# A bias pipeline run one group ahead, DMA zeros, fillers by length and joined multiplies in an attention kernel on one core

## The chip, the core and the metric

The kernel runs on one core of a Trainium2 chip. The metric is device time in microseconds (us), a median of several executions. Engines: PE (TensorE), PEld (its weight loads), DVE (VectorE), ACT (ScalarE), POOL (GpSimd), SP (SyncE). In the views, L411 is line 411 of that kernel, `<-` names what ended the idle time before an instruction, and PEclk is the clock granted to PE, 1.00 being full speed. The profiled executions were all fast. Three of the timed ones were slow (one of vrag_after, one of oldattn_loads_raw6, and one of the kernel before in the set with 404.1); the ratios leave them out, the medians and highest times don't.

A ratio is the mean time of one kernel's fast runs over that of the other's of the same rounds, so it is not quite the ratio of the medians beside it. The same kernel before took 404 to 405 us on some chips and 414 to 418 us on others, so times are compared only within one set of runs, which shared a chip.

## The reference

Attention for 8 batches, 8 heads, 576 positions and head size 64, with a bias that a small network computes from the distance of two positions; then each of the 4608 rows goes through the expert that its domain id names.

```python
x = (log1p(abs(i - j)) / log1p(max(i, 1)))[..., None]
bias = relu(x @ w1 + b1) @ w2            # hidden size 32, one bias for each head
scores = scale * q @ k.T + bias          # 576 x 576 for each batch and head
attn = exp(scores - max) / sum           # softmax
rows = (attn @ v)                        # 4608 rows of 512
for e in range(8):                       # 512 -> 1024 -> 512
    out[domain_id == e] = relu(rows[domain_id == e] @ w1[e]) @ w2[e]
```

## The kernel before

It has four stages: bias tables (0 to 69 us), attention (to 239), a hand-over in which rows are scattered to their experts and read back transposed (to 253), and the experts (to the end).

**Bias.** Nine groups of 16 hidden rows. DVE and ACT make the rows `hr`, PE multiplies them by the second layer, ACT evicts the result from PSUM as exp(bias) into `biasM`. Rows and outputs of one group stand next to each other in the program:

```python
for ib in range(9):
    hrl = []
    for k16 in range(16):                         # first layer: 16 rows
        ...                                       # on ACT for k16 in (3, 8, 13), else on DVE
        if ib > 0 or k16 > 7:
            next(route, None)                     # one step of the routing, on DVE
    for p in {5: (4, 0), 7: (1, 2)}.get(ib, ()):  at.take(0, p)
    for p in {4: (4, 0), 6: (1, 2), 8: (3,)}.get(ib, ()):  at.transposes(0, p)
    for jcs in ((0, 1), (2, 3), (4,)):            # second layer and evictions
        ...
at.make_vext(0)
at.take(0, 3)
```

**Attention.** A batch is 21 *units* of scores, counted from 0 here; each is 128 keys by 1024 scores at most. A unit is: score matmuls on PE, one exponential on ACT, and for most units a multiply by exp(bias) on DVE. Units of key block 3 (`RAW`, four a batch) instead get the bare bias added by two more PE matmuls, and cost DVE nothing. Between units PE gets *fillers*: a quarter of a PV product (`av`), or the transposes of a later batch. DVE copies the transposes (`take`), divides each finished PV product by its sums (`norm`) and copies V once a batch (`make_vext`). The next PV product reuses the same PSUM buffer, so it waits for the norm.

```python
while n < B * NU or av:
    b, ui = divmod(n, NU)
    new = self.scores(b, units[ui])               # PE scores, ACT exponential
    self.weight(job)                              # DVE multiply of the unit before
    job = new
    if b < B - 2 and ui == 1:   self.load_qk(b + 2); self.load_v(b + 2)   # load_qk loads the last rows too
    if b < B - 2 and ui == 9:   self.load_vrag(b + 2)
    if b < B - 1 and ui == 8:   self.make_vext(b + 1)
    budget = 4 if b >= B else 2 if n % 3 == 2 else 1
    while budget and (av or tr):                  # fillers: 1, 1, 2, 1, 1, 2, ...
        ...
```

**Zeros and ones.** POOL zeroes the ragged V tiles (`vrag`, for the last 64 keys), writes their columns of ones, zeroes the tiles of last rows (`last`), then issues its loads, and after them zeroes a tile with which one DMA of 9.25 MB fills the buffer that the rows are scattered to.

```python
for t in self.vrag:
    nc.gpsimd.memset(t, 0.0)
    nc.gpsimd.memset(t[0:64, :, 64:65], 1.0)
    nc.gpsimd.memset(t[64:128, :, 129:130], 1.0)
for t in self.last:
    nc.gpsimd.memset(t, 0.0)
...
at.start()                                        # the first loads
nc.gpsimd.memset(zv[:, :, 0:DM], 0.0)
nc.sync.dma_start(out=x_dram..., in_=zero.to_broadcast(...))
_phase_bias(tc, G, route, at)
```

The softmax here doesn't subtract the row's maximum and nothing guards it: scores larger than these inputs give would overflow.

## Time and profile before

The execution that was profiled took 404.8 us (span 403.1); the median given with it was 415.3.

| stage | from, us | to, us | what limits it |
|---|---|---|---|
| bias tables | 0 | 68.9 | DVE at first (busy for 10.9 of 11.0 us, 15 to 26), then ACT and PE in turn (37.6 and 32.4 of 42.0 us, 26 to 68) |
| attention | 68.9 | 238.7 | ACT (busy for 157.4 of 170.0 us), with PE close behind it (156.1) |
| hand-over | 238.7 | 252.7 | DMA and first transposes (PE waits 10.0 us for `xT`) |
| experts | 252.7 | 403.1 | PE (busy for 141.3 of 142.0 us, 253 to 395) |

"From" of attention is the start of the first score exponential, "to" the end of the last one; the experts begin with their first matmul. The eight batches, from first exponential to first exponential, lasted 21.6, 21.1, 21.3, 21.4, 21.2, 21.2, 21.2 and 20.7 us. The part of the profile that groups instructions by line has the two kinds of units beside each other. A row is: line, engine, operation, out<-in, shapes and count; then busy us and mean ns of one; then the idle time before them and who ended it.

```profile
L488 DVE TENSOR_TENSOR e<-e,biasM 128x1024 f16<-128x1024 f16 x96 | 63.2, 685 | 7.4 <-ACT e L483 7.0
L455 PE MATMUL sc<-biasM,idn 128*128 128x512 f16 x64 | 19.0, 378 | 3.1 <-ACT e L483 3.0
```

There are 96 multiplies (12 a batch by this tile) and 64 RAW matmuls (two for each of 32 RAW units). The change trades the one for the other.

### The profile page before, as it was taken

How to read it: one execution, taken by the hardware profiler on the slowest of the kernel's cores; microseconds unless marked ns; L12 is line 12 of the kernel's file. 1: busy time of each engine (PE TensorE's matmuls, PEld its weight loads, DVE VectorE, ACT ScalarE, POOL GpSimd, SP SyncE). 2: the span in 40 equal slices, each digit the busy share in tenths (PEclk: the TensorE clock that was granted, in tenths of full speed). 3: DMA queues.
4: the chain of work that ended last, by engine and by line, in shares of the span. 5: the costliest groups of instructions: out<-in, count | busy, mean ns of one | idle time of the engine just before them, and what ended most of it. 6: DMA issues, size and time to landing. Idle time of an engine off the chain costs nothing. (4 is left out here: it accounts for less than half of the span.)

```text
span 403.1 us, 9609 instructions
## 1 busy us (share of the span) xinstructions
PE 339.1 (84%) x3986; PEld 216.7 (54%) x3986; DVE 232.9 (58%) x486; ACT 256.7 (64%) x315; POOL 171.6 (43%) x232
## 2 busy tenths in 40 slices
PE   0357778889998999999897960999999999999991
PEld 0346666455656565656564540556565564655650
DVE  7999992878888888979797762020302213031220
ACT  8468989899999999999999960325042341514320
POOL 8660006603927639367470804044626323041321
PEclk9999985999999999999999996699999999999997
DMA  0999947980699998999492733959999999130311
GB/s 4 157 189 399 388 168 96 150 105 21 125 191 177 171 191 154 189 189 150 92 151 68 128 90 94 162 119 222 172 215 213 218 224 221 37 116 13 115 52 68
DMA packets 86068, 60.51 MB, mean 150 GB/s; under 512 B 43398, under 2 KB 76166, under 8 KB 86024
## 3 DMA queue, kind: packets, MB, share of 16 engines
q0 software_dynamic: 55808, 45.12, 65.6%
q1 hardware_dynamic: 30216, 14.78, 15.1%
q8 instruction: 31, 0.51, 0.5%
q14 instruction: 13, 0.11, 0.1%
HBM read 61.93 MB, written 24.70 MB: 215 GB/s over the span
## 5 line engine op out<-in xcount | busy, mean ns | idle before, releaser
L483 ACT ACTIVATE e<-sc 128x1024 f16<-128x1024 f32 x168 | 157.5, 994 | 12.5 <-PE sc L458 7.5
L670 DVE COPY res<-ops 128x512 f32<-128x512 f32 x40 | 27.7, 691 | 122.3 <-PE ops L667 122.3
L712 ACT ACTIVATE hT<-hps 128x640 f16<-128x640 f32 x56 | 39.4, 704 | 81.9 <-PE hps L693 81.9
L693 PE MATMUL hps<-xT,w 128*128 128x320 f16 x512 | 73.6, 306 | 10.0 <-DMA xT<-fire_x 10.0
L671 POOL DMA_INDIRECT out_dram<-res,ids x40 | 39.8, 996 | 93.4 <-DVE res L670 82.7
L667 PE MATMUL ops<-w,hT 128*128 128x512 f16 x320 | 70.4, 379 | 0.0
L693 PEld LDWEIGHTS <-w 128*128 128x128 f16 x512 | 51.2, 100 | 32.3 <-issue 10.1
L488 DVE TENSOR_TENSOR e<-e,biasM 128x1024 f16<-128x1024 f16 x96 | 63.2, 685 | 7.4 <-ACT e L483 7.0
L458 PE MATMUL sc<-qkT 64*128 64x512 f16 x256 | 50.3, 388 | 6.2 <-ACT e L483 5.4
L667 PEld LDWEIGHTS <-hT 128*128 128x128 f16 x320 | 31.3, 98 | 36.5
L505 PE MATMUL pu<-vext,e 128*128 128x65 f16 x1024 | 50.5, 194 | 0.0
L178 DVE TENSOR_SCALAR hr<-L,slope,nb 128x576 f16<-128x576 f16 x115 | 45.2, 459 | 0.0
L505 PEld LDWEIGHTS <-e 128*128 128x128 f16 x1024 | 43.7, 98 | 1.8 <-issue 0.8
L563 POOL DMA_INDIRECT fire_x<-xt,posi x32 | 34.5, 1077 | 18.9 <-issue 6.8
L196 PE MATMUL eb<-W2BIG,hr 128*128 128x32 f16 x576 | 26.4, 193 | 13.9 <-ACT hr L175 10.2
L501 PE MATMUL pu<-vrag,e 128*128 128x130 f16 x128 | 28.9, 226 | 5.2 <-DVE xl L549 2.1
L196 PEld LDWEIGHTS <-hr 128*128 128x128 f16 x576 | 22.1, 116 | 18.0 <-ACT hr L175 12.2
L563 POOL DMA_INDIRECT fire_x<-xl,posi x8 | 8.7, 1083 | 48.9 <-issue 26.6
L458 PEld LDWEIGHTS <-qkT 64*128 64x128 f16 x256 | 13.7, 93 | 28.6 <-issue 20.7
L635 POOL DMA_DIRECT2D w<-in_moe_w_dram x32 | 25.0, 810 | 4.5 <-DMA w<-in_moe_w_dram 4.5
L501 PEld LDWEIGHTS <-e 128*128 128x128 f16 x128 | 12.4, 97 | 24.2 <-issue 12.4
L388 POOL DMA_DIRECT2D qn<-in_q_dram x8 | 7.7, 964 | 40.8 <-PE pt L415 38.2
(116 smaller groups left out, 399.1 us busy)
## 6 DMA issues: line engine op xcount, KB each, us to landing
w<-in_moe_w_dram POOLq DMA_DIRECT2D x32, 512.0 KB, 9.5
fire_x<-zero SPq DMA_DIRECT2D x1, 9252.0 KB
qn<-in_q_dram POOLq DMA_DIRECT2D x8, 512.0 KB, 10.7
kn<-in_k_dram POOLq DMA_DIRECT2D x8, 512.0 KB, 8.8
vst<-in_v_dram POOLq DMA_DIRECT2D x8, 512.0 KB, 10.4
out_dram<-res,ids POOLq DMA_INDIRECT x40, 4.3
last<-in_q_dram POOLq DMA_DIRECT2D x16, 32.0 KB, 7.7
last<-in_k_dram POOLq DMA_DIRECT2D x16, 32.0 KB, 7.2
```

Of the source, the lines that this page charges most:

```text
L178: nc.vector.tensor_scalar(out=hr, in0=G.L4[:, c0: c0 + S], scalar1=G.slope[:, m: m + 1], scalar2=G.nb1[:], op0=AO.mult, op1=AO.max)
L196: nc.tensor.matmul(out=eb[:, lj, 32 * k16: 32 * k16 + 32], lhsT=rap(hr, jc, [[4, 128]]), rhs=G.W2BIG[:, 0:32], start=True, stop=True)
L458: mm(out=sc[:, h2, :], lhsT=self.qkT[b, p][hs[h2], 1, 128 * c: 128 * c + 128], rhs=self.qkT[b, p][hs[h2], 0, :], start=not raw, stop=True)
L483: nc.scalar.activation(out=ef[:, 0:n], in_=sf[:, 0:n], func=AF.Exp, bias=0.0, scale=0.125)
L488: self.nc.vector.tensor_tensor(out=job[0], in0=job[0], in1=job[1], op=AO.mult)
L501: mm(out=self.pu[:, c // 2, o: o + 130], lhsT=er[:, p % 2, 128 * c: 128 * c + 128], rhs=vr[:, p, :], start=True, stop=False, skip_group_ch ...
L505: mm(out=self.pu[:, c // 2, o + 65 * h2: o + 65 * h2 + 65], lhsT=self.e[b, ("m", p, j)][:, h2, 128 * c: 128 * c + 128], rhs=vx[:, 2 * p + ...
L563: inst = self.nc.gpsimd.indirect_dma_start(out=self.x_dram[:, :], out_offset=bass.IndirectOffsetOnAxis(ap=self.G.posi[0:n, c:c + 1], axis= ...
L667: nc.tensor.matmul(out=ops_, lhsT=hT[:, fc, t0: t0 + 128], rhs=G.w.w2(e, fc), start=(fc == 0), stop=(fc == 7))
L671: inst = nc.gpsimd.indirect_dma_start(out=out[:], out_offset=bass.IndirectOffsetOnAxis(ap=idx.bitcast(I32), axis=0), in_=res[:], in_offset ...
L693: nc.tensor.matmul(out=hps[:, i, 0:HC], lhsT=G.w.w1(e, dc)[:, 128 * fc: 128 * fc + 128], rhs=xT[:, dc, HC * hf: HC * hf + HC], start=(dc = ...
L712: nc.scalar.activation(out=hT[:, fc, :].rearrange("p (a b) -> p a b", a=2), in_=first(e, xT, ((fc, 0), (fc, 1))), func=AF.Relu, bias=0.0, ...
```

## The change

The intent: let ACT make rows while PE multiplies the group before; free POOL of memsets, so that loads go out earlier; give PE fillers by the time that a unit leaves, not by count; join two units in one multiply; and have two RAW units a batch instead of four. The core of the diff, with cuts marked:

```diff
-RAW = (3,)
+RAW = {3: 4}                      # block 3, from head 4 on: 2 units a batch
...
-        for ib in range(9):
+        def hidden(ib):            # 16 rows, 24 of 144 on ACT; routing steps in groups 1 and 2
...
+        hrl = hidden(0)
+        at.ones()
+        for ib in range(9):
+            after = hidden(ib + 1) if ib < 8 else None
+            ...                    # transposes of pairs 4, 0, 1 only; V copy
+                for _ in route:    # at ib == 8: the rest of the routing
+                    pass
+            outputs(ib, hrl)
+            hrl = after
...
         for t in self.vrag:
-            nc.gpsimd.memset(t, 0.0)
-            nc.gpsimd.memset(t[0:64, :, 64:65], 1.0)
-            nc.gpsimd.memset(t[64:128, :, 129:130], 1.0)
+            nc.sync.dma_start(out=t..., in_=G.zero...)
...
+    def ones(self):
+        for t in self.vrag:
+            self.nc.vector.memset(t[0:64, :, 64:65], 1.0)
+            self.nc.vector.memset(t[64:128, :, 129:130], 1.0)
...
     def start(self):
-        self.load_qk(0) ... self.load_vrag(1)
+        for b in range(2):
+            self.load_qk(b)
+            self.load_v(b)
+            self.load_last(b)
+            self.load_vrag(b)
...
+        self.joined = {("l", 0): 0, ("l", 1): 1}
+        for p in range(4):
+            n = 4 if all(2 * p < RAW.get(c, H) for c in range(4)) else 2
+            self.joined.update({("m", p, c): c % 2 for c in range(n)})
...
+                room = min(room + (0.5 if units[ui][0] == "x" else 0.91) - cost(units[ui]), 0.7)
...
-            if b < B - 2 and ui == 1:
+            if b < B - 2 and ui == 3:
                 self.load_qk(b + 2)
+            if b < B - 2 and ui == 7:
                 self.load_v(b + 2)
+                self.load_last(b + 2)
...
-            budget = 4 if b >= B else 2 if n % 3 == 2 else 1
-            while budget and (av or tr):
+            while av or tr:
+                lag = 2 if b >= B - 1 else 3
+                if av and room >= 0.34 - 0.15 and not (...):
...
+                    room -= 0.34
+                elif tr and room >= 0.52 - 0.15 and n >= NU * (tr[0][0] - 1) + 1:
+                    transpose()
+                    room -= 0.52
...
-            nc.gpsimd.memset(zv[:, :, 0:DM], 0.0)
             nc.sync.dma_start(out=x_dram..., in_=G.zero.to_broadcast(...))   # now before the loads have landed
```

The zero tile is now set by DVE, early, and the fill is issued as soon as that is done.

## The prediction

> **What bounds the kernel now.** I read the page's slices first, then busy time by stretch, then the waits inside each stretch, then single instructions in order of time.
>
> ```profile
> core 0: us, PE busy (x) PEld busy (x) DVE busy (x) ACT busy (x) POOL busy (x), PEclk, DMA share, GB/s
> 15.00:26.00 11.00, 6.43 (x131) 5.43 (x131) 10.90 (x38) 5.46 (x9) 6.74 (x10) 1.00 1.55 189
> 26.00:68.00 42.00, 32.44 (x670) 28.73 (x668) 36.06 (x95) 37.58 (x61) 7.39 (x10) 0.87 0.87 259
> ...
> 132.00:154.00 22.00, 20.48 (x315) 13.13 (x313) 19.14 (x36) 20.34 (x22) 11.43 (x14) 1.00 1.26 195
> ...
> 239.00:253.00 14.00, 1.86 (x38) 1.56 (x39) 3.90 (x14) 0.00 (x0) 5.02 (x5) 0.70 0.33 84
> 253.00:395.00 142.00, 141.25 (x832) 82.29 (x830) 27.66 (x40) 45.06 (x64) 50.01 (x53) 0.98 0.74 149
> ```
>
> Stretch by stretch: bias tables to 68 us (DVE full to 26, then ACT the busiest), attention from 69 to 239 (PE, ACT and DVE all near full), a hole of 14 us at the hand-over, then the expert layers, in which PE is never free. The last, 142 us of the 403, is not edited; its gain is nil. So the change lives in the first 253 us.
>
> In the bias stretch the chain goes round between ACT and PE:
>
> ```profile
> engine line waited for: us in total, times, longest us
> ...
> ACT biasM L214 <- PE eb L196: 12.7, 8, 5.3
> PEld L196 <- ACT hr L175: 12.2, 19, 1.9
> ...
> PE eb L196 <- ACT hr L175: 10.2, 18, 1.8
> ```
>
> PE waits for the rows that ACT makes, ACT waits for PE before it can evict. From group 3 the first eviction of a group starts at 37.80, 43.44, 49.06, 54.69, 60.33, 65.97: a period of 5.63 us, which is three rows (2.38) + wait (0.47) + evictions (2.11 + 0.76). DVE shows as busy there, but its rows start every 0.34 us when unhindered, 13 of them 4.5 us: it has some 1 us of slack a group.
>
> In attention I took the starts of the score exponentials one by one. Undisturbed they follow at 0.90 to 0.92 us; 20 of those and the short one (0.3) make 18.6 us a batch. The batches in fact start at 111.64, 132.96, 154.40, 175.61: 21.2 to 21.4 us. Of the missing 2.7 us, most follows waits of ACT for scores:
>
> ```profile
> 128.75 7.06 ACT L483 ACTIVATE e<-sc 128x1024 f16<-128x1024 f32 x7 [0.21 <-PE sc L458]
> 135.97 1.02 ACT L483 ACTIVATE e<-sc 128x1024 f16<-128x1024 f32 x1 [0.16 <-PE sc L458]
> 137.30 3.78 ACT L483 ACTIVATE e<-sc 128x1024 f16<-128x1024 f32 x4 [0.31 <-PE sc L458]
> 141.38 5.12 ACT L483 ACTIVATE e<-sc 128x1024 f16<-128x1024 f32 x5 [0.31 <-PE sc L458]
> ```
>
> So ACT is the wished-for bound, and PE, fed with fillers by count (one, one, two) and not by length, makes it late: the delayed slots are those after two fillers or after a RAW unit.
>
> [...] a row op that takes 0.42 us took 2.50 us at about 27 us, beside the 1.82 us POOL memset of the zero tile. [...] Here a 1024-element multiply lasts 0.69 us but starts every 0.60 when queued[...]. [...] here it was 0.58 in 250 to 260 us, after the 10 us wait for the first transposes. [...]
>
> **The change, part by part.**
> *Memsets.* POOL loses 1.82 + 0.29 (zero), 1.6 (three ragged V tiles), 1.9 (two last tiles): 5.6 us. Its first load starts at about 5 us and not 8.82. DVE gets the zero tile, an estimated 1 us, partly in the 0.8 us hole before its slopes. The 9.25 MB fill goes out at some 8 us instead of 28.5; at the 390 GB/s of the slices it needs 24 us and the first scatter is at 94 us, so it was hidden and stays hidden.
>
> *First layer ahead.* ACT rows fall from 29 to 24, DVE rows rise from 115 to 120 (+1.7 us). In program order the hidden rows of group n+1 stand before the outputs of n, so ACT works on rows while PE multiplies: the 0.47 wait goes. ACT a group: rows 3 or 2 (mean 2.5 x 0.79 = 2.0) + evictions 2.87 + about 0.1, since the eviction of block 3 is now two of half the size: 4.95 us instead of 5.63. But the start gets worse. The small routing matmul stands in PE's order before the first outputs, and its input is ready only at row 13 of group 1: 24 DVE rows at about 0.40[...], slopes 1.2, routing 1.6, ones 0.5, from 7 us: 20 us, where now PE begins at 15.3. Evictions of group 0 end at about 24. Then ACT has 18 rows (14.2) and eight groups of evictions (24): first score at 62.3 instead of 68.9. DVE, 94 rows from 22 us (32.0) and some 2.5 of the rest, ends its rows at 57, then 4.6 us of routing that was moved behind them; it does not bind. Gain 6.6 us.
>
> *Attention.* RAW units go from 4 to 2 a batch. Each RAW unit has two PE matmuls more (starts 0.52 us apart from the scores after them): PE loses about 1.0 us a batch. DVE gains two multiplies (2 x 0.60) and saves seven joins x 0.07: +0.7. Today's DVE batch by starts: 16 multiplies 9.6, short one 0.2, five copies 3.0, four norms 0.84 each 3.4, ragged norm 1.3, V copy 0.75: 18.2. New: 18.9 to 19.0, above ACT's 18.6. So DVE becomes the tightest engine, though ACT should no longer stand still long. I followed the new order of issue by hand: the five double buffers are always free in time, and at most one or two fillers stand between scores. Two spots remain in which a double multiply (1.13) delays a norm and the norm delays the next PV group, by an estimated 0.3 us each. I take 19.9 us, between the 19.0 floor and today's 21.2: 1.35 x 8 = 10.8 us. The two transposes moved out of the bias stretch fall in the first batch, where no PV filler competes.
>
> *Tail.* The ragged PV group of the last batch now comes before the end of the scores. Today the last exponential ends at 238.7 and the last PV group starts at 240.36, behind the ragged norm; it can start at once. About 1.5 us off the hand-over; the scatters, transposes and the half-clock start stay.
>
> Sum: 6.6 + 10.8 + 1.5 = 18.9, which I round up to 19.8 because the fewer POOL memsets should also shorten early DVE ops. Taken from the timed 415.3 and not from the 404.8 of the profiled run: 395.5.
>
> **Rivals.** (a) DVE takes over fully: its multiplies, norms and copies queue behind one another, PV waits, and a batch stays at 20.7. DVE at 19.1 of 22 speaks for it, its three idle stretches a batch (up to 1.47 us) against. Gain from attention 4, time about 402. (b) The start jams: the memset of ones on DVE stands behind the ragged V loads and DVE waits for DMA, or for the fill[...]. Up to 7 us lost, cancelling the bias gain: about 402 too. Against: the loads are small. Both together, about 408. (c) All works: 19.2 a batch and no start penalty, 16 + 9 + 2: 388. (d) The bias gain is eaten because DVE starts attention behind with the moved routing; the order of 57 + 5 against 62 says that it just fits.
>
> **Range and chances.** One rival alone gives 402, both 408, the best case 388. Range 386 to 406. The threshold of 2% is 407.0 us; that needs both rivals or an unseen stall: 6%. Slower by 2% needs over 27 us against me: 1%.
>
> **What would show it.** First exponential at 62 +- 2; group period near 5.0; PE's first bias matmul near 20; batches at 19.9 +- 0.5; RAW matmuls 32 and not 64, mean PE wait of ACT small; DVE busy share in attention above 90%; first expert matmul 11 to 13 us after the last exponential; the expert stretch 142 us still. I am wrong if batches stay over 20.7, or if DVE stands before the ones for microseconds.

Four of its figures, as the traces have them. The clock that was 0.58 in 250 to 260 us of before is the one granted to PE. The longest row op on DVE took 2.50 us in before and 0.67 in after, the median 0.42 and 0.43. The 0.07 us that a join saves is the author's estimate; in the trace of after, what follows a double multiply (1.22 us long) on DVE without a wait starts 1.13 to 1.14 us after it, and what follows a single one (0.69) 0.61 in after and 0.60 in before: 1.20 to 1.22 for two singles against 1.13 for a double. The zero tile took DVE 0.92 us (after, from 1.93).

## The result

The changed kernel took 452.76 us (450.3 to 455.4, 4 runs) against 414.51 (413.1 to 417.0) for the kernel before on the same chip: a ratio of 1.092 [1.083, 1.100]. It is slower by 9%, and right in its output.

The busy times of the stretches of the changed kernel:

```profile
core 0: us, PE busy (x) PEld busy (x) DVE busy (x) ACT busy (x) POOL busy (x), PEclk, DMA share, GB/s
...
12.00:58.00 46.00, 0.00 (x0) 0.00 (x0) 0.44 (x4) 1.22 (x1) 10.07 (x15) 1.00 1.24 282
58.00:104.00 46.00, 32.26 (x772) 30.52 (x773) 43.83 (x132) 37.99 (x73) 0.00 (x0) 0.85 0.01 3
104.00:290.00 186.00, 157.42 (x2323) 102.13 (x2318) 151.84 (x239) 156.43 (x168) 100.59 (x124) 0.95 0.89 132
290.00:302.00 12.00, 1.74 (x34) 1.53 (x35) 2.73 (x10) 0.00 (x0) 4.82 (x5) 0.58 0.35 91
302.00:444.00 142.00, 140.42 (x832) 81.97 (x831) 27.67 (x40) 45.06 (x64) 50.58 (x54) 0.99 0.75 152
```

From 12 to 58 us almost nothing computes: DVE is busy for 0.44 us, PE for none, ACT for 1.22, while the DMA engines move 282 GB/s. The bias stage proper then runs from 58 to 104 us, and attention lasts 186 us where it lasted 170. Each stage by the marks of the table above:

| | before | after | difference |
|---|---|---|---|
| first exponential | 68.9 | 103.9 | +35.0 |
| attention | 169.8 | 185.8 | +16.0 |
| hand-over | 14.0 | 12.3 | -1.7 |
| experts to the end | 150.4 | 149.5 | -0.9 |
| span | 403.1 | 451.4 | +48.3 |

(The two profiled executions ran on different kinds of chip, so the 48.3 isn't the 38.3 between the medians; the experiments below separate the parts.)

The list of waits of the changed kernel names the hole:

```profile
PE app L305 <- DVE rowtot L302: 64.4, 1, 64.4
ACT biasM L221 <- PE eb L197: 52.5, 1, 52.5
DVE vrag L411 <- DMA vrag<-in_v_dram: 46.1, 2, 37.0
```

PE and ACT wait long, but only as the next in the chain: the routing matmul (`app`) is the first in PE's order and needs a row total that DVE computes after its memsets. The root is the third line: DVE waited 46.1 us for loads of V. In order of time, the fill, the loads and the memsets (start, duration, engine, line, instruction, idle before and releaser):

```profile
8.16 1.14 SPq L876 DMA_DIRECT2D fire_x<-zero  x1
12.25 0.06 DVE L410 MEMSET vrag<- 64x4 f16 x1
15.61 1.25 POOL L425 DMA_DIRECT2D last<-in_q_dram  x2 [8.01 <-DMA last<-zero]
18.06 1.26 POOL L439 DMA_DIRECT2D vrag<-in_v_dram  x2
...
39.53 0.88 POOL L417 DMA_DIRECT2D kn<-in_k_dram  x1 [13.77 <-DMA vst<-in_v_dram]
49.28 0.06 DVE L411 MEMSET vrag<- 64x4 f16 x1 [36.97 <-DMA vrag<-in_v_dram]
...
58.60 0.06 DVE L411 MEMSET vrag<- 64x4 f16 x1 [9.14 <-DMA vrag<-in_v_dram]
```

Line 411 is the memset of the lower half's column of ones. It takes 0.06 us and waits 36.97 for the first batch's ragged V load and 9.14 for the second's. The load writes columns 65 to 128 of those partitions, the memset column 129: they share no byte, but the load stands first in the program, and the wait is there. (The upper half's memset, line 410, didn't wait; why the two are treated differently the trace doesn't say.) The ones are needed by PE only in attention. The loads in turn are late: POOL stood 8.01 us for the zeros of `last`, and later 13.77 for an earlier load, while the fill was under way: from 16 to 44 us its queue moved 9.01 MB and the loads' queue 0.79; from 46 to 56, with the fill through, the loads' queue moved 1.73. The DMA zeros were meant to send the loads out earlier. That came true of the first load (4.54 us and not 8.82), but not of the last rows, which went out at 15.61 where they had gone at 10.83.

In attention, the exponentials of batch 4 (ACT) answer to the four lines of before:

```profile
198.26 3.92 ACT L523 ACTIVATE e<-sc 128x1024 f16<-128x1024 f32 x4 [0.46 <-PE sc L497]
202.39 3.77 ACT L523 ACTIVATE e<-sc 128x1024 f16<-128x1024 f32 x4 [0.21 <-PE sc L497]
208.08 1.02 ACT L523 ACTIVATE e<-sc 128x1024 f16<-128x1024 f32 x1 [1.92 <-PE sc L497]
210.42 1.94 ACT L523 ACTIVATE e<-sc 128x1024 f16<-128x1024 f32 x2 [1.31 <-PE sc L497]
```

In the lines of before, ACT's waits were 0.16 to 0.31 us. Now two runs of four follow without a wait inside, and then come waits of 1.92 and 1.31 us. In the groups by line the trade of RAW units reads as predicted, with 48 double multiplies of 1.225 us (and 16 single ones beside them) and 32 RAW matmuls:

```profile
L534 DVE TENSOR_TENSOR e<-e,biasM 128x2048 f16<-128x2048 f16 x48 | 58.8, 1225 | 1.1 <-ACT e L523 0.9
L494 PE MATMUL sc<-biasM,idn 128*128 128x512 f16 x32 | 11.1, 432 | 2.4 <-ACT e L523 2.4
```

### The profile page after: what moved, and what is told of

Its sections match the earlier page's. It is cut to its first block, busy times and chain, and to the rows that moved or that the text cites. A ratio compares the mean times of both kernels' runs of the same rounds, so it can differ in the third digit from the quotient of the medians.

```text
span 451.4 us, 9441 instructions
## 1 busy us (share of the span) xinstructions
PE 331.8 (74%) x3954; PEld 216.3 (48%) x3954; DVE 235.9 (52%) x459; ACT 250.9 (56%) x318; POOL 173.2 (38%) x219
## 5 line engine op out<-in xcount | busy, mean ns | idle before, releaser
L764 PE MATMUL hps<-xT,w 128*128 128x320 f16 x512 | 72.6, 303 | 9.5 <-DMA xT<-fire_x 9.5
L534 DVE TENSOR_TENSOR e<-e,biasM 128x2048 f16<-128x2048 f16 x64 | 69.0, 1090 | 1.1 <-ACT e L523 0.9
L551 PE MATMUL pu<-vext,e 128*128 128x65 f16 x1024 | 53.7, 200 | 3.8 <-DVE e L534 3.5
L497 PE MATMUL sc<-qkT 64*128 64x512 f16 x256 | 51.4, 396 | 2.8 <-ACT e L523 2.0
L551 PEld LDWEIGHTS <-e 128*128 128x128 f16 x1024 | 46.6, 102 | 6.6 <-DVE e L534 4.9
L609 POOL DMA_INDIRECT fire_x<-xt,posi x32 | 43.4, 1358 | 10.2 <-issue 8.8
L221 ACT ACTIVATE biasM<-eb 128x256 f16<-128x256 f32 (+2 forms) x32 | 16.4, 586 | 52.5 <-PE eb L197 52.5
L180 DVE TENSOR_SCALAR hr<-L,slope,nb 128x576 f16<-128x576 f16 x120 | 42.1, 434 | 1.2 <-PE eb L201 1.1
L547 PE MATMUL pu<-vrag,e 128*128 128x130 f16 x128 | 29.5, 231 | 13.3 <-DVE xt L578 8.6
L547 PEld LDWEIGHTS <-e 128*128 128x128 f16 x128 | 12.7, 99 | 28.9 <-issue 11.6
```

The source lines that it names most:

```text
L180: nc.vector.tensor_scalar(out=hr, in0=G.L4[:, c0: c0 + S], scalar1=G.slope[:, m: m + 1], scalar2=G.nb1[:], op0=AO.mult, op1=AO.max)
L497: mm(out=sc[:, h2, :], lhsT=self.qkT[b, p][hs[h2], 1, 128 * c: 128 * c + 128], rhs=self.qkT[b, p][hs[h2], 0, :], start=not raw, stop=True)
L534: self.nc.vector.tensor_tensor(out=job[0], in0=job[0], in1=job[1], op=AO.mult)
L547: mm(out=self.pu[:, c // 2, o: o + 130], lhsT=er[:, p % 2, 128 * c: 128 * c + 128], rhs=vr[:, p, :], start=True, stop=False, skip_group_ch ...
L551: mm(out=self.pu[:, c // 2, o + 65 * h2: o + 65 * h2 + 65], lhsT=self.e[b, ("m", p, j)][:, h2, 128 * c: 128 * c + 128], rhs=vx[:, 2 * p + ...
L609: inst = self.nc.gpsimd.indirect_dma_start(out=self.x_dram[:, :], out_offset=bass.IndirectOffsetOnAxis(ap=self.G.posi[0:n, c:c + 1], axis= ...
```

## The experiments

Two questions: what makes the start stall, and why is attention longer although every engine has less or little more to do in it? For the start the theories were *memset behind loads* (order in the program alone) and *fill in the way* (the 9.25 MB is under way while the loads are). For attention they were *joining* (theory A in the expectations: the joined multiplies are too coarse), *DVE* (B, later D and "quantity": with two RAW units DVE has too much to do), *dealing* (C: fillers by length are worse than by count), *backlog* ("order": what stands on DVE in front of the norm), and, later, *loads* (the new places of the loads).

All results, in order of the runs. "Exp" is the start of the first exponential, "attention" the time from it to the end of the last one, and "batch" a typical batch without a stall, in us from the profiled execution (those of both_unjoin, both_vext_takes and both_all hold a stretch of half clock, see below). Kernels of one call shared the runs of the kernel before, whose median stands beside.

| kernel | exp | attention | batch | median | before | ratio [95%] |
|---|---|---|---|---|---|---|
| before, profile | 68.9 | 169.8 | 21.2 | | | |
| after | 103.9 | 185.8 | 22.5 to 23.9 | 452.8 | 414.5 | 1.092 [1.083, 1.100] |
| vrag_after | 66.4 | 181.4 | 22.5 | 414.1 | 415.6 | 0.999 [0.991, 1.007] |
| fill_late | 78.1 | 184.6 | 22.5 | 425.9 | 415.6 | 1.024 [1.018, 1.029] |
| both | 61.0 | 182.8 | 22.5 | 408.1 | 415.6 | 0.982 [0.977, 0.987] |
| both_unjoin | 60.9 | 194.4 | 24.6 | 419.4 | 415.6 | 1.008 [1.003, 1.014] |
| both_oldattn | 60.9 | 177.7 | 21.2 | 404.3 | 404.5 | 1.001 [0.998, 1.004] |
| both_olddeal | 60.9 | 181.1 | 22.0 | 407.5 | 404.5 | 1.007 [1.004, 1.011] |
| both_olddeal_unjoin | 60.8 | 180.3 | 22.3 | 407.2 | 404.5 | 1.007 [1.004, 1.010] |
| both_vext14 | 60.6 | 180.3 | 21.6 | 404.5 | 404.5 | 1.002 [0.998, 1.006] |
| oldattn_loads_back | 61.1 | 172.3 | 21.3 | 399.2 | 404.1 | 0.988 [0.983, 0.994] |
| oldattn_loads_join | 61.0 | 172.7 | 21.2 | 398.7 | 404.1 | 0.986 [0.981, 0.991] |
| both_loads_back | 60.7 | 183.1 | 22.2 to 23.7 | 407.4 | 404.1 | 1.008 [1.003, 1.013] |
| both_loads_vext | 60.8 | 179.8 | 21.6 | 404.7 | 404.1 | 1.002 [0.996, 1.007] |
| both_vext_takes | 60.7 | 200.0 | 25.2 | 423.7 | 417.7 | 1.013 [1.007, 1.019] |
| oldattn_loads_raw6 | 60.9 | 185.5 | 22.2 | 412.0 | 417.7 | 0.986 [0.980, 0.992] |
| oldattn_loads_route | 61.1 | 189.1 | 21 to 25 | 414.0 | 417.7 | 0.992 [0.987, 0.997] |
| both_all | 60.6 | 198.1 | 25.3 | 422.9 | 417.7 | 1.014 [1.008, 1.020] |
| before_again | 69.2 | 169.8 | 21.2 | 404.5 | 404.8 | 0.999 [0.993, 1.004] |
| join_again | 61.3 | 172.5 | 21.2 | 398.7 | 404.8 | 0.984 [0.981, 0.987] |

All gave right results. The sets with 414.5, 415.6 and 417.7 ran on the slower kind of chip. A ratio found there is not that of the other kind: `both` and both_loads_back differ little and took 408.1 and 407.4 us, but their ratios are 0.982 and 1.008, because the kernel before took 415.6 and 404.1. In the set with 417.7 the traces show stalls of 2 to 4 us at changing places in attention; its totals are read only within the set. The cause of the stalls is open, as no trace of the kernel before was taken there.

### The start: vrag_after, fill_late, both

**vrag_after** puts the ragged V loads behind the ones in the program and changes nothing else:

```diff
             self.load_last(b)
-            self.load_vrag(b)
...
         at.ones()
+        at.load_vrag(0)
+        at.load_vrag(1)
```

> The loads of the ragged V tiles are issued after the memset of the ones and no longer before it; nothing else moves. Theory (the memset of the ones stands behind those loads, and DVE behind the memset): DVE goes on at about 12.5 us where it went on at 58.9, first bias matmul near 20 us, first exponential at 62 to 66 us where it was 103.9, time near 412 us. Rival (it is the zero fill that holds up all loads, and q, k and the last rows of batch 0, which landed at 25 to 47 us, are needed by the transposes of group 5 anyway): PE then waits for them and the time only falls to about 430 us. The batches of the attention stay at 22 to 24 us under both.

The first exponential came at 66.4 us, 37.5 earlier, and the ratio fell from 1.092 to 0.999. DVE's own timeline has the first rows after the memsets:

```profile
13.15 0.77 DVE L180 TENSOR_SCALAR hr<-L,slope,nb 128x576 f16<-128x576 f16 x2
```

DVE resumed at 13.15 instead of 58.91 (the memsets now waited 0.28 us, for the zeros). With the order mended, nearly all of the stall was gone.

**fill_late** leaves that order and gives the fill a tile of its own, which POOL zeroes after the loads are issued, as in the kernel before:

```diff
+            zero2 = G.bsb.tile([P, 1, 4 * XW], F16, tag="zero2", name="zero2")
+            nc.gpsimd.memset(zv2[:, :, 0:DM], 0.0)      # after at.start()
             nc.sync.dma_start(out=x_dram...,
-                              in_=G.zero.to_broadcast(...))
+                              in_=zero2.to_broadcast(...))
```

> The zero fill gets its own tile again, set by POOL behind the loads as in the kernel before; the ones stay behind the ragged loads. Theory (the fill slows the loads on which the ones wait): the second ragged load lands at about 22 us, the DVE stall ends there and not at 58.6, first exponential at 68 to 72 us, time near 418 us. Rival (the loads are slow for another reason, such as POOL waiting for the tiles that the DMA sets to zero): the stall stays over 20 us and the time over 430 us.

```profile
22.37 0.06 DVE L411 MEMSET vrag<- 64x4 f16 x1 [10.07 <-DMA vrag<-in_v_dram]
...
32.87 0.06 DVE L411 MEMSET vrag<- 64x4 f16 x1 [10.33 <-DMA vrag<-in_v_dram]
```

The same two memsets waited 20.4 us and not 46.1. So the order is enough for a stall of 20 us, and the early fill makes it 46.

**both** has the two edits. It is the base of all later kernels.

> Both edits together. If the start was all that the forecast of the bias stretch missed: first exponential at 61 to 63 us, group period 4.9 to 5.0 us, time near 410 us. If the fill was no matter once the ones are out of the way, this equals vrag_after within 2 us; if the fill also delays the transposes, this is 3 to 8 us faster than vrag_after.

First exponential 61.0. Against vrag_after, the fill alone still costs 5.4 us (66.4 to 61.0) once the memsets are out of its way: in vrag_after PE stood 8.22 us before a transpose of the last rows (the profile names no releaser) and 1.07 before the next, for their load; POOL had issued these loads from 38.98 to 48.83 us, where both has no such wait. POOL's long stops for an earlier load (12.59 us in vrag_after, 13.77 in the changed kernel) come in these two alone, which have the early fill; in the other eighteen traces none of that kind in the first 58 us is over 2.7 us. The start is settled: 46.1 us of stall from the order, lengthened by the fill, and 5.4 us from the fill by another way.

### Attention: both_unjoin and both

Even `both` has batches of 22.5 us where the prediction had 19.9 and the kernel before had 21.2. **both_unjoin** multiplies every unit by itself again:

```diff
-        self.joined = {("l", 0): 0, ("l", 1): 1}
-        for p in range(4): ...
+        self.joined = {}
```

> As both, with every multiply of one unit (18 single buffers). Theory A (the double multiply of 1.2 us delays the norm, PE stands behind the norm, ACT starves): batches fall from 22 to 24 us to 21 or less, time near 398 us. Theory B (DVE has too much work in a batch, so that singles, which cost 0.4 us a batch more, make it worse): batches 0.3 to 0.5 us longer than in both, time 2 to 4 us above it.

It made batches longer, 24.6 us, and the ratio rose from 0.982 to 1.008. Theory A falls: with two RAW units and this dealing, joining saves time. By how much is less clear. Theory B had expected 0.3 to 0.5 us a batch and not 2, but a stretch of half clock (below; the mean granted clock was 0.947 in this run and 0.972 in `both`) lies in batches 2 to 5 of both_unjoin; in the two full batches without one, 1 and 6, the difference is 1.7 us (22.4 against 20.7) and 0.4 (22.9 against 22.5). That speaks for DVE as the engine that PE waits for. DVE's timeline of `both` in batch 4 shows how:

```profile
156.72 1.22 DVE L536 TENSOR_TENSOR e<-e,biasM 128x2048 f16<-128x2048 f16 x1
157.85 1.28 DVE L474 COPY qkT<-pt 128x1024 f16<-128x1024 f16 x2
159.05 1.21 DVE L536 TENSOR_TENSOR e<-e,biasM 128x2048 f16<-128x2048 f16 x1
160.18 0.69 DVE L446 COPY vext<-vst 128x2048 f16<-128x2048 f16 x1
160.78 1.22 DVE L536 TENSOR_TENSOR e<-e,biasM 128x2048 f16<-128x2048 f16 x1
161.92 0.20 DVE L579 RECIPROCAL rz<-pu 128x8 f32<-128x8 f32 x1
162.21 0.69 DVE L580 TENSOR_TENSOR xt<-pu,rz 128x512 f16<-128x512 f32 x1
```

It is one row without a gap: multiply, two transposes' copies, multiply, the V copy, multiply, and only then the norm (the last two lines). PE's last matmul of that PV product ended at 160.15, but the norm began at 161.92. PE's next PV product reads:

```profile
162.96 0.23 PE L549 MATMUL pu<-vrag,e 128*128 128x130 f16 x1 [1.54 <-DVE xt L580]
```

and, as scores stand behind it in PE's order, ACT's next exponential starts 1.62 us late. No engine is full on average (DVE is busy for 19.1 of a 22.5 us batch); its work is bunched in front of the one instruction that PE needs. At 160.15 the end of a multiply, the V copy and another multiply stood ahead of the norm, and it ran behind them, at 161.92.

In the changed kernel a stretch of half clock came behind this wait. Two windows around it in batch 4:

```profile
203.10:206.50 3.40, 1.86 (x35) 1.19 (x34) 3.31 (x6) 3.06 (x4) 2.80 (x2) 1.00 1.13 170
206.50:209.90 3.40, 3.40 (x40) 2.16 (x37) 2.67 (x5) 1.02 (x1) 1.61 (x2) 0.50 1.37 208
```

PE was busy for 1.86 of 3.40 us, with 1.54 us as its longest idle stretch, and for the next 3.40 its clock was 0.50. The same came again at 230.4 and 254.3 (PE busy for 1.86 and 1.91 of the 3.40 us before), and these batches last 23.9 us where two without it last 22.4 and 22.5 (batch 0 has it too, at 117.7). (both_loads_back, below, mean clock 0.959, has it in batches 3, 4 and 6, of 23.3 to 23.7 us, and not in 2 and 5, of 22.2 and 22.4.) In `both` no half clock followed the very wait shown above: PE was busy for 2.01 of the 3.50 us from 159.40, and the clock was 1.00 in them and in the next 3.40. What separates the two cases is not shown. (PE's ends are modelled, so these shares are rough.)

### Attention: RAW units, dealing and the V copy

**both_oldattn** puts the attention back, four RAW units, fillers by count and single multiplies, but leaves the new places of the loads:

```diff
-RAW = {3: 4}
+RAW = {3: 0}
-        self.joined = {("l", 0): 0, ("l", 1): 1} ...
+        self.joined = {}
-                if av and room >= 0.34 - 0.15 and not (...):
+                if av and not (...):          # with budget = 2 if n % 3 == 2 else 1
```

> The mended start and the new bias stretch, with the attention as it was before: four RAW units, single multiplies, fillers dealt by count. If the bias stretch is worth what the forecast gave it and nothing else acts: first exponential at 61 us, batches 21.2 to 21.4 us as in the kernel before, time 407 to 409 us. If the new bias stretch leaves something behind (the routing moved to the end of DVE's list, two transposes moved into batch 0): batch 0 over 22.5 us, time near 410 us.

Batches were at 21.2 again, with three exceptions, 23.9 (batch 0), 25.5 (batch 4) and 22.1 (batch 7, otherwise 20.7). So it is the attention edits that make the batches longer. But the total was 404.3 against 404.5: attention took 177.7 us against 169.8, so the 8 us won at the start had gone, all in those three batches. In batch 4 unit 2 took 4.25 us. The waits of the stretch have the cause, which was a surprise:

```profile
PEld L449 <- DMA last<-in_q_dram: 2.5, 2, 2.1
...
PE ptl L449 <- DMA last<-in_q_dram: 1.8, 1, 1.8
```

PE's transposes waited for the last rows of Q: the change loads them at unit 7 behind V instead of unit 1, and POOL, held up by other loads (2.92 us before one of them), issued them late.

**both_olddeal** and **both_olddeal_unjoin** keep two RAW units, with fillers by count; the second has single multiplies.

> Mended start, two RAW units and double multiplies kept, fillers dealt by count again. Theory C (the dealing by length puts two transposes and three double multiplies in front of the norm on DVE): batches 21 us or less, the wait of 1.5 us before the second PV group gone, time 396 to 400 us. Rival D (the two more multiplies and the doubling are too much for DVE in any order): batches 22 us or more, time 405 us or more.

> Mended start, two RAW units, single multiplies, fillers by count: against both_oldattn only the number of RAW units differs. If PE was what made the batches of before long: batches 20.5 us, time 400 us. If DVE is near its limit (18 single multiplies, 19.4 us of work by starts): batches 21.7 us or more, time 412 us.

Typical batches were 22.0 and 22.3 us, totals the same (1.007 both). So joining is worth about 0.3 us a batch under the old dealing; and with two RAW units the old dealing does no worse than the new (22.0 against 22.5, though on different chips), so theory C falls and what was expected under rival D (22 us or more) came. Neither reaches the 21.2 of four RAW units. both_olddeal_unjoin and both_oldattn differ in nothing but the number of RAW units and ran on one chip: two instead of four cost about 1 us a batch in this order (22.3 against 21.2).

**both_vext14** moves the V copy out of the bunch of units 7 to 11:

```diff
-            if b < B - 1 and ui == 8:
+            if b < B - 1 and ui == 14:
                 self.make_vext(b + 1)
```

> As both, with the copy of V (0.6 us of DVE) at unit 14 and no longer at unit 8. Backlog theory (DVE works without a gap from unit 2 to the norm, so each 0.1 us taken from that list comes off the wait of PE): slot 11 falls from 2.66 to about 2.06 us, batches from 22.5 to 21.9, time near 403.5 us. Rival (the norm waits for PE or for the exponentials): slot 11 and the time unchanged.

From unit 11 to the next exponential `both` needed 2.47 us (median of batches 1 to 7), this kernel 1.76; its batches were 21.6. On one chip the same pair of kernels comes again below (both_loads_back and both_loads_vext): 2.36 against 1.76 at unit 11, attention 183.1 against 179.8. PE's wait for the norm in batch 2 of the two, with the V copy in front of it and without:

```profile
117.43 0.23 PE L549 MATMUL pu<-vrag,e 128*128 128x130 f16 x1 [1.54 <-DVE xt L580]
116.13 0.23 PE L549 MATMUL pu<-vrag,e 128*128 128x130 f16 x1 [0.94 <-DVE xt L580]
```

The copy itself lasts 0.69. This is the direct test of the bunching, and it holds. But batch 4 again had a stall at unit 2 (4.21 us), and the total was no better than before's.

Batch 1 of `both` shows the order at work without any edit. DVE has the same instructions in it as in batch 4 (19.0 us of work against 19.1), but there the norm follows the V copy at once, one multiply earlier, and PE has two sets of transposes to do meanwhile and not one:

```profile
93.25 0.69 DVE L446 COPY vext<-vst 128x2048 f16<-128x2048 f16 x1
93.86 0.20 DVE L579 RECIPROCAL rz<-pu 128x8 f32<-128x8 f32 x1
```

PE waits for no norm, and the batch lasts 20.7 us, less than the 21.1 of the kernel before. Batch 1 of all seven kernels with two RAW units, joined multiplies, fillers by length and no held-back copies lasts 20.7 to 20.9 us. (PE has six PV matmuls fewer in it, of 164.)

### The loads: four kernels

**oldattn_loads_back** is both_oldattn with the loads where they were, and the last rows ahead of V:

```diff
-            if b < B - 2 and ui == 3:
+            if b < B - 2 and ui == 1:
                 self.load_qk(b + 2)
-            if b < B - 2 and ui == 7:
+                self.load_last(b + 2)
                 self.load_v(b + 2)
-                self.load_last(b + 2)
-            if b < B - 2 and ui == 11:
+            if b < B - 2 and ui == 9:
                 self.load_vrag(b + 2)
```

(The expert weights also went from unit 14 back to 13, so the two moves are not told apart.) **oldattn_loads_join** has joined multiplies besides; **both_loads_back** and **both_loads_vext** are `both` and both_vext14 with these loads.

> As both_oldattn, but the loads of batch b+2 go out where they did before (q, k, last rows, V at unit 1, ragged V at unit 9, weights at unit 13). Theory (the last rows, loaded since the change at unit 7 and behind V, come too late for the transposes; slot 2 of batch 4 was 4.25 us for that): slot 2 is back at 1.2 us in batch 4, batch 4 at 21.3, 4 us less than both_oldattn, so 0.985 to 0.99 of the kernel before. Rival (the late batch comes from the expert weights' loads): unchanged, 1.00.

> As oldattn_loads_back, with double multiplies for blocks 0 and 1 and the ragged pair (4 RAW units, so five pairs a batch; 10 single and 4 double buffers). If joining saves its 0.07 us apiece and nothing else changes: batches 0.2 to 0.4 us shorter, 2 to 3 us less than oldattn_loads_back. If the later start of the first half of a pair matters: batches longer than 21.3 us.

> As both, with the loads where they were before. If late loads are one part of the loss: the two batches over 23 us in both (5 and 7) and batch 0 fall to 22.5, time 3 to 4 us less than both, which is 0.975 of the kernel before on the same chip; the other batches stay at 22.5 us, since their wait is for the norm.

> As both_loads_back, with the copy of V at unit 14. Batches 21.6 to 21.7 us as in both_vext14 but without its late batch 4; 6 to 7 us less than both_loads_back over eight batches; still no faster than oldattn_loads_back, whose batches are 21.2 to 21.3 us.

The two with the old attention had no stalled batch and gained: 0.988 and 0.986, whose intervals overlap, so joining at four RAW units isn't shown to be worth anything. With two RAW units the old loads did not help: 407.4 us where `both` took 408.1, and 404.7 where both_vext14 took 404.5. On this one chip the attention of after (183.1) and of before (172.3) stand beside each other: the edits to attention cost 10.8 us. In both_loads_vext the stall even came again in batch 5 (25.9 us, unit 2 at 3.92), again with PE waiting for the last rows of Q. So with the loads moved back the stall was gone from one kernel and not from another; what else brings those loads late is open.

### The last sets

**both_vext_takes** also holds back DVE's copies of the transposes of units 5 and 6 to unit 10, to clear the way for the norm; **oldattn_loads_raw6** has six RAW units; **oldattn_loads_route** spreads the rest of the routing over batch 0; **both_all** combines vext, takes, loads and routing with two RAW units.

```diff
+            if b >= B or ui not in (5, 6):
+                flush()                      # both_vext_takes, both_all: copies wait until unit 10
...
-RAW = {3: 4}
+RAW = {3: 0, 2: 4}                           # oldattn_loads_raw6
...
-                for _ in route:
-                    pass
+                    if b == 0 and ui > 1:    # oldattn_loads_route, both_all: in late()
+                        next(route, None)
```

> As both_vext14, with DVE's copies for the transposes of units 5 and 6 held back to unit 10, behind the norm. Order theory (the work queued on DVE in front of the norm is what PE waits for): slot 11, 2.66 us in both and 1.76 in both_vext14, falls below 1.2 us, batches 20.8 to 21.1 us, below the 21.2 of the old attention; 4 to 6 us less than both_vext14 in time. Quantity theory (DVE has simply too much to do with two RAW units): the wait reappears at another slot and batches stay at 21.5 us or more.

> As oldattn_loads_back with six RAW units (block 2 of heads 4 to 7 as well), so two multiplies a batch less on DVE and four matmuls a batch more on PE. With two RAW units a batch was 22.2 us, with four 21.2. If DVE is the limit in that order too: 20.6 us a batch, 4 us less. If PE is: 22 us or more, 6 us more than oldattn_loads_back.

> As oldattn_loads_join, with the 14 remaining steps of the routing on DVE spread over the units of batch 0, where the change has them in one piece in front of the first copy of V. If that piece of 4.6 us is what makes batch 0 long (24.9 us in oldattn_loads_join against 21.6 in the kernel before): batch 0 falls to 22 to 23 us, time 2 to 3 us less, 0.98 of the kernel before. If the two transposes moved into batch 0 are the cause: no difference over 1 us.

> The changed attention with everything mended: ragged loads behind the ones, late fill, loads where they were, copy of V at unit 14, late copies, routing spread. If the order theory holds: batches 20.8 us, batch 0 near 22, time 0.975 of the kernel before or less. If DVE's quantity binds: no better than oldattn_loads_route, 0.985 or more.

This chip was of the slow kind, and its scattered stalls make the batches hard to read. Still: both_vext_takes has batches of 25.2 us and more, in which unit 10 takes 3.6 to 4.6 us, since the held copies keep their PSUM buffers and PE's next transposes stand behind them:

```profile
PE pt L449 <- DVE qkT L474: 17.5, 6, 3.3
```

Taking work away from in front of one instruction had put it in front of another, as had been expected under the quantity theory. (A stretch of half clock lies in each of batches 1 to 6, too; the mean granted clock of this run was 0.945.) With six RAW units the undisturbed batches were 22.1 to 22.2: PE is then the engine that is short (busy for 20.8 us of batch 1, DVE for 17.2). With the old dealing and single multiplies that makes 22.3 us for two, 21.3 for four and 22.2 for six, each from another chip, so only the minimum at four is read from it. Batch 0 with the routing spread was 23.8 against 24.9 (oldattn_loads_join, another chip): perhaps 1 us, not shown. both_all was 1.014.

Two more variants, four RAW units with fillers by length (joined or single), could not be built: their order of issue came to a deadlock. So four RAW units were tried only with fillers by count.

**before_again** is the kernel before, unedited, and **join_again** is oldattn_loads_join, on one more chip.

> The kernel before, unedited, for its trace. On two chips of this study it took 404 us, on two others 415 to 418, while the changed attention took 407 to 408 on one of each kind. If this call falls on a slow chip: the 10 us more lie in the attention (batches over 22 us, at slots that differ from batch to batch) and not in the bias stretch or the 142 us of the experts. On a fast chip: 404 us, batches 21.2 us.

> The best of the variants (oldattn_loads_join) once more on another chip, beside the kernel before: 0.98 to 0.99 of it if the gain of the bias stretch holds on any chip; first exponential at 61 us.

join_again took 398.7 us against 404.8: 0.984 [0.981, 0.987]; before_again, 0.999, shows that the comparison is sound. The attention of join_again:

```profile
61.00:234.00 173.00, 159.85 (x2355) 101.29 (x2354) 143.42 (x238) 157.35 (x169) 94.47 (x123) 0.98 0.93 142
```

The first exponential came 7.9 us earlier than in before_again (61.3 against 69.2), attention lasted 2.6 more (172.5 against 169.8), all of it in batch 0 (24.6 against 21.8), and the rest 0.6 more; that is the 4.7 us between the spans (402.6 and 397.9). With oldattn_loads_back, from which it can't be told apart, it is the best version found, and it keeps of the change the bias stage ahead, the zeros by DMA and the joined multiplies. What the zeros by DMA are worth by themselves no run shows.

## Why the prediction was wrong

**The start.** The step that failed is rival (b), "The start jams": it named this very memset behind these very loads, and gave it "Up to 7 us lost" with "Against: the loads are small". The trace of after has 46.1 us. In the sum for the start it is the term "ones 0.5", which holds no wait: PE's first bias matmul, forecast for 20 us, came at 64.46. Their size (32 KB each) was not what made these loads late: the first batch's were issued at 18.06 and the second's from 50.70, behind the zeros of `last` (8.01 us) and other loads, and up to about 45 us the fill was under way (9.01 MB against 0.79 in 16 to 44 us). The other failed step is "it was hidden and stays hidden": the fill's own end was indeed not waited for, but it slowed others, by 5.4 us in the mended kernel and by some 26 us in the unmended one (46.1 against 20.4 in fill_late). By how much a fill slows the loads beside it no one had measured, and in the sum it counts as nothing.

**The bias stage.** Once mended, it was right. Predicted were PE's first bias matmul near 20, the first exponential at 62.3 and a group period of 4.95; `both` has 19.2 and 61.0, and in the changed kernel the first evictions of the groups (65.68, 70.80, 75.04, 80.03, 84.26, 89.24, 93.47, 98.47) are 4.68 apart on average, as in `both` (20.42 to 53.21). The gain of 6.6 us was 7.9; the four smaller evictions, for which 0.1 us more was set down, took 2.03 us where the three of before took 2.11.

**Batch 0.** Rival (d), that moved work would eat the gain, was set aside with "it just fits". It doesn't: the V copy and two transposes' copies stand behind the routing that ran to 63.3 us on DVE (oldattn_loads_back, first exponential at 61.1), and batch 0 is 1.5 to 3.8 us longer in every mended kernel (23.3 to 25.3 where before had 21.6 to 21.8). How much of that is the routing and how much the moved transposes is not shown.

**Attention.** The step that failed is "Two spots remain ... by an estimated 0.3 us each. I take 19.9 us". DVE's sum, 18.9 to 19.0 us, was right (19.1 busy of 22.5). What was not worked out is where in the batch that work lies. The norm runs behind an unbroken row of double multiplies, transposes' copies and the V copy; unit 11 took 2.66 us, 1.75 over the 0.91 of an undisturbed one, where 0.3 was said, and smaller losses lie at units 3 (0.55), 7 (0.35) and 12 (0.3 to 0.6): together some 3 us on the 18.6 of exponentials, and short waits make up the rest of the 22.5. Predicted was a gain of 10.8 us; measured, on the faster kind of chip, is a loss of 13.3 (both_loads_back, 183.1, against before_again, 169.8), of which some 2.5 are batch 0.

Rival (a), "DVE takes over fully", had the mechanism (multiplies, norms and copies queue behind one another, PV waits) but expected 20.7, a gain; its size was wrong too. That the bunching makes the wait is shown by both_vext14 (0.6 us less at unit 11 on one chip, and 3.3 of attention, for one copy moved). (The 3.3 us also hold three stretches of half clock on the one side and a stall of batch 5 on the other; the 0.6 us of wait is the clean figure.)

Two RAW units are not too few for DVE in every order: batch 1, with the same work on DVE, took 20.7 us. But no order tried kept batches 2 to 6 below 21.6, and in both_olddeal and both_vext_takes what the rival forecast came; what an order that holds batch 1's pace would give is open. The 19.9 us was reached by no batch.

**Not foreseen.** The late loads of the last rows (2 to 4 us in one batch of some kernels), and the half clock after PE's waits (0.50 for 3.40 us; batches 4 to 6 of the changed kernel, which have it, last 23.9 us, and 2 and 3, which don't, 22.4 and 22.5).

**The tail** was right: "About 1.5 us off the hand-over", measured 14.0 to 12.3 in the changed kernel and 12.4 in `both`, lost again with the old dealing (14.2 in join_again). The experts didn't change, as said.

**The scale.** The profile of before came from an execution of 404.8 us, and its gain was taken from 415.3. These are two kinds of chip, as the sets of runs show, and a ratio of one kind isn't that of the other (`both` above). A sum of stages should be set against the run that it was read from. Nor were the 0.9 us by which 18.9 was rounded up to 19.8 worked out from anything.

## What to carry to other kernels

Before moving an instruction to another engine, ask which earlier instruction of the program touches its tile, and when that one can be done; here a 0.06 us memset put behind loads waited 37 us and its twin 9, and with the loads put behind them the memsets waited 0.28. An engine's busy sum doesn't say that another can be fed (DVE was busy for 19.1 of 22.5 us, and PE waited 1.54 for one norm): list what stands ahead of the one instruction that the other engine waits for. And a background transfer with a late deadline was not free here: the early fill cost 5.4 us even with the memsets out of its way, so ask what is needed early while it is under way.
